# Hash attention and gated feed-forward on one core: the first batch issued from one written list

## The chip, the cores and the metric

The kernel runs on one core of one Trainium2 chip. TensorE (PE) does matrix products, VectorE (DVE) and ScalarE (ACT) do elementwise work and may read PSUM, GpSimd (POOL) does elementwise work on SBUF only, SyncE (SP) issues most of the DMAs. The metric is the device time of one execution in microseconds; less is better. The profile gives a span, from the first to the last instruction of one profiled execution, and that execution's own time.

## The reference

Four batches of eight heads, 768 tokens, head size 64. Each token of q and of k gets a bucket from the signs of six projections; a query attends only to keys in its own bucket. The attention output of a batch (768 tokens x 512) goes through a gated feed-forward layer.

```python
q_bits = (np.einsum('bhsd,dk->bhsk', q, proj) > 0)      # six bits per token, k alike
mask = q_bucket[:, :, :, None] == k_bucket[:, :, None, :]
scores = np.where(mask, scale * q @ k.T, -1e9)
attn = exp(scores - max) / (sum + 1e-9);  x = attn @ v  # 4 x 768 tokens, 512 wide
g = x @ w_gate;  val = x @ w_val
out = x + sigmoid(x @ w_res) * ((gelu(g) * val) @ w_out)
```

## The kernel before, in words

Work goes by *pairs* of heads, four pairs to a batch, sixteen in all (pair 0 to 15). For a pair and a side (0 is q, 1 is k), a tile `ld` holds 12 token groups of 128 tokens (six of either head) by 64 values; the code calls these groups stripes where it handles fewer than six. The path of one side of a pair is:

- `load` or `load_head` (DMA, issued on SP), `tr` (DVE, 32x32 block transposes into `t32`), and `cast` (POOL or ACT, to bf16 in `nat`).
- the hash: for pair 0 `hash_one` (two fp32 matmuls for one head) and `bits_one` (DVE, a transpose and a threshold); for the later pairs `hash_mm` (fp32 matmuls, two or four jobs side by side), `hash_tok` (DVE, one transpose into `ht`) and `bits` (thresholds of 32 partitions each, on DVE or partly on POOL). The six signs stand in `nat` beside the values, so that a plain product of q and k with these 71 rows gives the score with the mask in it.
- the turn to 71 x 128: in batch 0 `turn_pe` (six PE transposes into PSUM) and `turned` (a copy to `aug`); in later batches `turn`, a transposing DMA.
- `vals_a` and `vals_s` (POOL): v in bf16 with a column of ones, and its sum over the token groups.

The attention of a pair is nine *slots*. `scores` makes 1024 columns of scores in one of two PSUM buffers `sp` (1024 columns on PE, L384) and one exponential of 128x1024 on ACT (L389) into one of four `e` buffers. `values`, two slots later (LAG), multiplies `e` by v in eight small matmuls (L358). Slots 0 to 3 and half of slot 4 are the first head of the pair. At the end of a head a `preset` matmul adds a tiny multiple of the sum of v (L330), and `finish` (DVE) divides into `x_tok`. Then x is transposed into `x_sb`, by DMA for pairs 0 and 1 of batch 0, by PE (`x_turn`) for pairs 2 and 3.

After the 36 slots of a batch, `gate_val` runs twelve steps m: product with w_gate, product with w_val (L403, two `sp` buffers), gelu on ACT (L420), product of both on DVE (L423). Its first three quarters of m=0 (`begun`) can start before the last pair is there. `project` (the residual gate and w_out, L435 and L449) is spread over the slots of the next batch, so batches 1 to 3 have feed-forward matmuls to fill PE in their slots and batch 0 has none.

Order is written by hand (`manual_schedule`): each engine executes its instructions in the order in which the program issues them, and waits only for what it needs. The loop over slots issues, for slot s: the scores, the pieces in `side_pe[s]`, the values of slot s-2, then the pieces in `side_work[s]`. Pieces are filed under slots by `at`, `pe`, `turns_pe`, `hash_pe` and `loads`, and under steps of `gate_val` by `gv`. POOL also issues the weight loads (`load_w`), SP the loads of q, k and v, the transposing DMAs and the stores.

Where the change and the prediction touch it: the start of pair 0 (L461 to L487), the fillings of batch 0 (L541 to L572), the next batch's hashes (`hashed`, L517; for pairs 4 and 5 of batch 1 it runs in three quarters before and one quarter inside step m=0, L638 and L639; for pairs 6 and 7 in step m=6, L596; in the later batches half before and half inside m=0, L646 and L647), and the `e` buffers (L388).

## Time and profile before

| what | us |
|---|---|
| three runs | 346.02 to 346.23, median 346.22 |
| the profiled execution: its own time | 346.3 |
| its span | 344.6 |
| stretch 0 to 7.9 (start): PE busy | 6.38 of 7.90 |
| stretch 7.9 to 47.1 (slots of batch 0): PE, ACT, DVE, POOL busy | 37.47, 33.85, 30.37, 33.20 of 39.20 |
| stretch 47.1 to 83.2 (`gate_val` of batch 0): PE busy | 35.73 of 36.10 |
| stretch 83.2 to the end: PE busy | 255.56 of 261.40 |

The stretches come from the view that gives each engine's busy time between two moments. Busy times of PE include the latency of each matmul, so that a chain of matmuls that follow one another with short waits still looks full; what a step costs PE is read from one start to the next. A row of the timeline is: start, duration, engine, line, operation, output<-input, shape, count, and in brackets the idle time before it with what ended it. A row of the groups ends with busy time, mean duration in ns, and the idle time before, with its releaser.

### The profile page before, as it was taken

What the parts mean: (1) busy time and instruction counts of PE and PEld (TensorE: products, weight loads), DVE (VectorE), ACT (ScalarE), POOL (GpSimd) and SP (SyncE); (2) the same over time, 40 slices, a digit from 0 to 9 for tenths busy, and PEclk for the clock granted to TensorE, in tenths of its full rate; (3) what the DMA queues carried; (4) which work ended last, traced back from release to release, by engine and by line L of the source; (5) the groups of instructions that cost most, each with busy time, mean ns of one, the idle gap of its engine ahead of it and who ended that gap; (6) DMA issues with size and microseconds to landing.
All of it is one profiled execution on the core that took longest, in us unless ns stands there. A gap on an engine that the chain in (4) does not pass through costs nothing.

```text
span 344.6 us, 7573 instructions
## 1 busy us (share of the span) xinstructions
PE 335.1 (97%) x3076; PEld 204.8 (59%) x3124; DVE 192.0 (56%) x405; ACT 206.9 (60%) x232; POOL 86.2 (25%) x162
## 2 busy tenths in 40 slices
PE   8999999999999999999999999999999999999996
PEld 5667665655666665655566665656566665555444
DVE  7877757755344866657344684657344444434343
ACT  3889973226999962224999983222899994322220
POOL 4779940343055000260044200143020000000000
PEclk9999999999999999999999999999999999999999
DMA  7939999969476832527466632724420040000012
GB/s 216 374 73 239 243 269 200 158 85 218 132 166 186 219 107 67 103 48 137 93 187 196 216 101 86 137 49 91 91 79 32 32 101 30 30 3 0 32 61 92
DMA packets 71251, 42.90 MB, mean 124 GB/s; under 512 B 49456, under 2 KB 68272, under 8 KB 71216
## 3 DMA queue, kind: packets, MB, share of 16 engines
q1 hardware_dynamic: 64800, 37.17, 42.3%
q0 software_dynamic: 6336, 5.24, 10.1%
q8 instruction: 24, 0.39, 0.4%
q14 instruction: 11, 0.09, 0.1%
q10 hardware_dynamic: 80, 0.00, 0.0%
HBM read 29.36 MB, written 6.29 MB: 103 GB/s over the span
## 4 chain that ended last, share of the span: by engine, by line
PE 88%; ACT 4%; DVE 2%; DMA 2%; issue 2%; SPq 1%; POOL 0%; DVEq 0%; ACTq 0%
PE sp L403 36%; PE fps L449 17%; PE sp L384 15%; PE av L358 8%; PE rps L435 6%; ACT e L389 4%; PE hs L205 3%; DMA ld<-in_k_dram 2%; PE pt L259 1%; DVE o L455 1%; DVE nat L224 0%; SPq L96 0%; DVE o L452 0%; DVE ht L215 0%; PE av L333 0%
## 5 line engine op out<-in xcount | busy, mean ns | idle before, releaser
L389 ACT ACTIVATE e<-sp 128x1024 bf16<-128x1024 f32 x144 | 143.7, 1027 | 13.8 <-PE sp L384 8.2
L420 ACT ACTIVATE gt<-sp 128x768 bf16<-128x768 f32 x48 | 38.9, 811 | 93.0 <-PE sp L403 93.0
L384 PE MATMUL sp<-aug,aug 71*128 71x256 bf16 (+1 forms) x384 | 86.1, 325 | 1.1 <-ACT e L389 0.6
L449 PE MATMUL fps<-wo,hh 128*128 128x512 bf16 (+2 forms) x286 | 74.7, 361 | 1.6
L423 DVE TENSOR_TENSOR hh<-gt,sp 128x768 bf16<-128x768 bf16 x48 | 45.8, 954 | 50.4 <-PE sp L403 45.2
L403 PE MATMUL sp<-x_sb,wg 128*128 128x256 bf16 (+1 forms) x373 | 70.4, 324 | 0.7
L403 PE MATMUL sp<-x_sb,wv 128*128 128x512 bf16 (+1 forms) x379 | 70.6, 325 | 0.4 <-DVE hh L423 0.2
L358 PEld LDWEIGHTS <-e 128*128 128x128 bf16 x1152 | 53.3, 97 | 28.9 <-issue 1.2
L358 PE MATMUL av<-va,e 128*128 128x65 bf16 x1152 | 58.7, 193 | 0.1
L403 PEld LDWEIGHTS <-wv 128*128 128x128 bf16 x384 | 37.5, 98 | 25.1 <-issue 0.3
L403 PEld LDWEIGHTS <-wg 128*128 128x128 bf16 x384 | 36.6, 98 | 26.3 <-issue 3.0
L449 PEld LDWEIGHTS <-hh 128*128 128x128 bf16 x312 | 28.1, 97 | 22.3 <-issue 0.5
L452 DVE SCALAR_TENSOR_TENSOR o<-th,fps 128x512 f32<-128x512 f32 (+2 forms) x26 | 16.8, 645 | 35.9 <-PE fps L449 31.4
L384 PEld LDWEIGHTS <-aug 71*128 71x128 bf16 x384 | 29.4, 97 | 10.9 <-issue 2.1
L184 POOL TENSOR_SCALAR nat<-ld 128x768 bf16<-128x768 f32 (+1 forms) x16 | 14.6, 912 | 76.6 <-DMA aug<-nat 73.2
L281 POOL TENSOR_TENSOR v<-ldv 128x384 f32<-128x384 f32 x16 | 16.0, 1001 | 66.3 <-DMA ldv<-in_v_dram 66.1
L194 DVE STREAM_TRANSPOSE t<-ld 128x768 f32<-128x768 f32 (+1 forms) x34 | 30.9, 914 | 0.9 <-DMA ld<-in_q_dram 0.7
L337 DVE COPY av<-av 128x390 f32<-128x390 f32 x24 | 13.6, 567 | 29.4 <-PE av L333 29.4
L435 PE MATMUL rps<-wr,x_sb 128*128 128x512 bf16 x90 | 25.3, 378 | 0.2
L439 ACT ACTIVATE th<-rps 128x512 f32<-128x512 f32 x24 | 14.2, 593 | 18.5 <-PE rps L435 18.5
L224 DVE TENSOR_SCALAR nat<-htp 32x72 bf16<-32x72 f32 x96 | 21.9, 229 | 1.7
L455 DVE SCALAR_TENSOR_TENSOR o<-o,x_tok 128x512 f32<-128x512 f32 (+2 forms) x26 | 18.4, 709 | 0.9
(61 smaller groups left out, 190.5 us busy)
## 6 DMA issues: line engine op xcount, KB each, us to landing
ldv<-in_v_dram SPq DMA_DIRECT2D x16, 384.0 KB, 5.3
out_dram<-o SPq DMA_DIRECT2D x23, 256.0 KB, 2.0
ld<-in_q_dram SPq DMA_DIRECT2D x15, 384.0 KB, 5.3
ld<-in_k_dram SPq DMA_DIRECT2D x15, 384.0 KB, 6.2
wg<-in_moe_w_gate_dram POOLq DMA_DIRECT2D x4, 384.0 KB, 7.8
wv<-in_moe_w_val_dram POOLq DMA_DIRECT2D x4, 384.0 KB, 9.7
wo<-in_moe_w_out_dram POOLq DMA_DIRECT2D x3, 512.0 KB, 6.3
wr<-in_moe_w_res_dram POOLq DMA_DIRECT2D x1, 512.0 KB, 12.6
```

The costliest lines, as they stand in the source:

```text
L194: nc.vector.transpose(t32[p, side][:, sl].rearrange("p c h n -> p (c h n)"), raw[p, side][:, sl].rearrange("p c d -> p (c d)"))
L224: engs[a % len(engs)].tensor_scalar(nat_of(x)[32 * a:32 * a + 32, :, D:D + NBITS], ht[32 * j:32 * j + 32, :, NBITS * a:NBITS * (a + 1)], 0 ...
L358: nc.tensor.matmul(av[p, hi][:, qt, :], e[:, off:off + P], va[:, hi, jt, 0:D + 1], start=first, stop=(p >= HP and jt == T - 1), skip_group ...
L384: nc.tensor.matmul(sp[:, off:off + nq * P], ks[0:KA, hi * T + jt, :], qs[0:KA, hi * T + qt0:hi * T + qt0 + nq, :], start=True, stop=True)
L389: nc.scalar.activation(e, sp, AF.Exp, scale=float(ALPHA))
L403: nc.tensor.matmul(sp[:, c0:c1], w[:, kk, bass.ts(m, P)], xs[:, kk, c0:c1], start=(kk == 0), stop=(kk == KM - 1))
L420: nc.scalar.activation(gt, sp[:, 0:S], AF.Gelu)
L423: nc.vector.tensor_mul(hidden[b][:, m, :], gt, ps[1][:, 0:S])
L435: nc.tensor.matmul(rps, x_sb[b][:, kk, t, :], wr[:, kk, :], start=(kk == 0), stop=(kk == KM - 1))
L449: nc.tensor.matmul(fps[:, cs], hh[:, m, bass.ts(t, P)], wo[:, m, cs], start=(m == 0), stop=(m == KF - 1))
L452: nc.vector.scalar_tensor_tensor(o[:, cs], th[:, cs], 1.0, fps[:, cs], op0=ALU.add, op1=ALU.mult)
L455: nc.vector.scalar_tensor_tensor(o3, o3, 0.5, x_tok[b][:, k0:k1, t, :], op0=ALU.mult, op1=ALU.add)
```

## The change

Batch 0 no longer runs through the slot loop. A list `PLAN` names every step of it in order, one engine's instruction order being what the list gives that engine. `('S', c)` is the scores and exponential of slot c, `('V', c)` its values, `('w',)` a weight load, `'v'`, `'s'`, `'p'` stand for DVE, ACT and POOL. `BESIDE` and `BESIDE_GV` do the same for the steps beside `gate_val` of batch 0. What differs in the order:

- Pair 0 is hashed, turned and copied in runs of stripes (k 0 to 2, q 0 to 4, q 4 to 6, k 2 to 6, then the second heads whole). Three of the copies ahead of the first exponential, and the copy of the second head's q behind the third, are on ACT. The eight warming matmuls stand together, and the two short ones that stood between the first transposes are gone.
- The exponentials of batch 0 go into a ring of nine, in place of four buffers, and the values are placed by the list, not two slots behind.
- The loads of pair 1 stand ahead of the first v; later loads, casts and thresholds have new places (the thresholds of pair 3's q are all on POOL).
- The hash of pairs 2 and 3 runs in one piece after S12. The hash of pairs 4 and 5 moves from behind the slots to S34 and S35 (three quarters and one quarter). The hash of pairs 6 and 7 moves from step m=6 into step m=0.
- The first part of `gate_val` (`gv` 0) stands after the last values, where before it stood ahead of them.
- Tokens that `hash_tok` writes to SBUF leave a gap of one group after every four, so `bits` reads them as 3 x 4 x 6 in place of 12 x 6.
- In batches 1 and 2 the hash runs whole inside step m=0.

```diff
+PLAN = [
+    ('load', 1, 0), ('load', 1, 1), ('load_v', 0), ('load', 2, 0), ('load_v', 1), ('load', 2, 1),
+    ('load', 3, 0), ('proj', 's', 'pssp'), ('cast', 0, 1, 'p', 0, 6), ('cast', 0, 0, 'p', 6, 12),
+    ('proj', 'w', 'pppp'), ('fill', 1, 256), ('tr', 0, 0, 0, 4), ('cast', 0, 0, 's', 0, 6), ('fill', 7),
+    ('hash1', 0, 0, 0, 4, 'av'), ('tr', 0, 0, 4, 6), ('tr', 0, 1, 2, 6), ('tr', 0, 1, 0, 2),
+    ('cast', 1, 0, 'p'), ('hash1', 0, 1, 0, 2, 'av'), ('tr', 0, 0, 6, 12), ('bits1', 0, 0, 0, 4),
+    ('hash1', 0, 1, 2, 6, 'w1'), ('hash1', 0, 0, 4, 6, 'w0'), ('bits1', 0, 1, 0, 2),
+    ('cast', 0, 1, 'p', 6, 12), ('turn', 0, 1, 0, 2, 'f'), ('load', 3, 1), ('bits1', 0, 1, 2, 6),
+    ('copy', 0, 1, 0, 2, 's'), ('load_v', 2), ('turn', 0, 0, 0, 4, 'r'), ('hash1', 0, 0, 6, 12, 'av'),
+    ('bits1', 0, 0, 4, 6), ('copy', 0, 0, 0, 4, 's'), ('tr', 0, 1, 6, 12), ('bits1', 0, 0, 6, 12),
+    ('cast', 1, 1, 'p'), ('turn', 0, 1, 2, 6, 'f'), ('va', 0), ('turn', 0, 0, 4, 6, 'r'),
+    ('copy', 0, 0, 4, 6, 's'), ('copy', 0, 1, 2, 6, 'v'),
+    ('S', 0), ('tr', 1, 0), ('turn', 0, 0, 6, 12, 'av'),
+    ('S', 1), ('load', 5, 0), ('hash1', 0, 1, 6, 12, 'av'),
+    ('S', 2), ('tr', 1, 1), ('bits1', 0, 1, 6, 12), ('vs', 0), ('cast', 2, 0, 'p'), ('tr', 2, 0),
+    ('copy', 0, 0, 6, 12, 's'),
+    ('S', 3), ('hash', (1,), 0), ('vs', 1), ('hash', (1,), 1), ('hash', (1,), 2),
+    ('turn', 0, 1, 6, 12, 'f'), ('copy', 0, 1, 6, 8, 'v'), ('hash', (1,), 3), ('V', 0), ('load_v', 3),
+    ('S', 4), ('tokens', (1,)), ('copy', 0, 1, 8, 12, 'v'), ('va', 2),
+    ('S', 5), ('V', 1), ('load', 4, 1), ('V', 2), ('V', 3), ('bits', 1, 0, 'v'),
+    ('S', 6), ('bits', 1, 1, 'v'), ('va', 1), ('turn', 1, 0, 0, 6, 'r'), ('tr', 3, 0), ('V', 4),
+    ('S', 7), ('turn', 1, 1, 0, 6, 'f'), ('cast', 2, 1, 'p'), ('copy', 1, 0, 0, 6, 'v'), ('V', 5),
...
+    ('S', 11), ('load_v', 4), ('V', 9), ('copy', 1, 1, 6, 12, 'v'),
+    ('S', 12), ('hash', (2, 3), 0), ('hash', (2, 3), 1), ('hash', (2, 3), 2), ('hash', (2, 3), 3),
+    ('va', 3),
+    ('S', 13), ('load', 5, 1), ('finish', 0, 1), ('tokens', (2, 3)),
+    ('S', 14), ('w',), ('bits', 2, 0, 'vvvp'), ('V', 10), ('V', 11), ('load', 4, 0),
+    ('bits', 2, 1, 'pv'), ('w',), ('turn', 2, 0, 0, 6, 'r'),
+    ('S', 15), ('copy', 2, 0, 0, 6, 'v'), ('V', 12), ('turn', 2, 1, 0, 6, 'f'), ('cast', 3, 1, 'p'),
+    ('bits', 3, 0, 'p'),
+    ('S', 16), ('cast', 3, 0, 'p'), ('copy', 2, 1, 0, 6, 'v'), ('V', 13), ('tr', 5, 0),
+    ('S', 17), ('turn', 2, 1, 6, 12, 'f'), ('load', 7, 1), ('cast', 4, 1, 'p'), ('V', 14),
...
+    ('S', 19), ('bits', 3, 1, 'pv'), ('V', 16),
+    ('S', 20), ('V', 17), ('turn', 3, 0, 0, 6, 'r'), ('load', 6, 1),
+    ('S', 21), ('load', 6, 0), ('V', 18), ('w',),
+    ('S', 22), ('tr', 5, 1), ('turn', 3, 1, 0, 6, 'f'), ('V', 19), ('copy', 3, 0, 0, 6, 'v'),
...
+    ('S', 34), ('va', 4), ('hash', (4, 5), 0), ('hash', (4, 5), 1), ('hash', (4, 5), 2),
+    ('S', 35), ('hash', (4, 5), 3), ('V', 32), ('V', 33), ('tr', 6, 0), ('V', 34), ('tr', 7, 0),
+    ('V', 35), ('gv', 0), ('finish', 3, 1), ('preset', 4, 0), ('tr', 7, 1), ('xturn', 3),
+    ('tokens', (4, 5)), ('gv', 1), ('repeat', 4, 0), ('gelu',), ('load_v', 6),
+]
+BESIDE = [('hash', (6, 7), 0), ('hash', (6, 7), 1), ('hash', (6, 7), 2), ('hash', (6, 7), 3)]
...
-            ht = sm_pool.tile([P, HT, 32], FP32, tag="ht", name="ht")
...
+            ht = hh_pool.tile([P, 3, HT // 3 + 1, 32], FP32, tag="ht", name="ht")[:, :, 0:HT // 3]
...
-    def hash_one(p, side, hi, pool, tag):
+    def hash_one(p, side, c0, c1, tag):
...
-    def turn_pe(p, side, hi, tag=None, pool=mm_ps):
+    def turn_pe(p, side, c0, c1, tag, pool=mm_ps):
...
-        e = e_pool.tile([P, 1024], BF16, tag="e", name="e")
+        if p < HP:
+            if c == 0 and p == 0:
+                ring.append(hh_pool.tile([P, NE, 1024], BF16, tag="hh", name="ering"))
+            e = ring[0][:, (p * NCH + c) % NE]
+        else:
+            e = e_pool.tile([P, 1024], BF16, tag="e", name="e")
...
+    for m, name, *args in BESIDE_GV:
+        gv(0, m, lambda name=name, args=args: STEP[name](*args))
+    for name, *args in PLAN:
+        STEP[name](*args)
+    gate_val(0, begun, lambda: [STEP[name](*args) for name, *args in BESIDE])
+    mlp.append(project(0))
...
-                    hashed(ps, 0, 2)
-                    gate_val(b, begun, lambda: hashed(ps, 2, 4))
+                gate_val(b, begun, lambda: hashed(ps))
```

233 lines of the change are left out of this document (101 added, 132 removed), and 16 rows, old and new, of the table PLAN.

## The prediction

> **What bounds the kernel now.** The page comes first: PE is called busy for nearly all of the span, so anything that is to help must take work or waiting off PE.
>
> ```profile
> span 344.6 us, 7573 instructions
> PE 335.1 (97%) x3076; PEld 204.8 (59%) x3124; DVE 192.0 (56%) x405; ACT 206.9 (60%) x232; POOL 86.2 (25%) x162
> ```
>
> That share is an average and includes latency, so I went on to the groups of the stretch 8 to 47, the slots of batch 0, and to ACT's timeline there.
>
> ```profile
> L389 ACT ACTIVATE e<-sp 128x1024 bf16<-128x1024 f32 x36 | 34.5, 1025 | 5.6 <-PE sp L384 5.3
> ```
>
> ```profile
> 8.58 4.08 ACT L389 ACTIVATE e<-sp 128x1024 bf16<-128x1024 f32 x4 [0.89 <-PE sp L384]
> 13.65 1.02 ACT L389 ACTIVATE e<-sp 128x1024 bf16<-128x1024 f32 x1 [1.00 <-PE sp L384]
> ...
> 37.26 10.46 ACT L389 ACTIVATE e<-sp 128x1024 bf16<-128x1024 f32 x11 [0.16 <-PE sp L384]
> 47.73 1.28 ACT L633 ACT_TABLE_LOAD   x1
> ```
>
> The 36 exponentials start at 8.58 and end at 47.72 (37.26 + 10.46). ACT stood still for 5.6 us before them, 0.89 of it ahead of the first; so some 4.7 us between the first and the last are ACT waiting for scores. In an unbroken run one exponential follows the other after 10.46 / 11 = 0.951.
>
> What a slot costs PE is read from starts:
>
> ```profile
> 6.35 0.50 PE L259 MATMUL pt<-ident,nat 128*71 128x128 bf16 x6 [0.46 <-DVE nat L242]
> 6.68 0.38 PE L150 MATMUL wps<-warm 128*128 128x256 bf16 x2
> ...
> 7.24 0.87 PE L234 MATMUL hs<-t,projs 128*128 128x192 f32 x4
> 7.94 0.60 PE L384 MATMUL sp<-aug,aug 71*128 71x512 bf16 x2
> ...
> 17.16 0.60 PE L384 MATMUL sp<-aug,aug 71*128 71x256 bf16 x3
> 17.60 0.41 PE L358 MATMUL av<-va,e 128*128 128x65 bf16 x8
> 17.85 0.60 PE L384 MATMUL sp<-aug,aug 71*128 71x512 bf16 x3
> ```
>
> Scores 0.44, values 0.25, together 0.69; the turn of a head's side 0.33; one head's hash for pair 0 0.70. Against ACT's 0.951, PE has 0.26 a slot for turns, hashes and presets. The two are close, so a hash in one piece starves ACT, and waiting for ACT idles PE. Behind the slots PE runs without a break; there a microsecond less of PE work is a microsecond of the total.
>
> ```profile
> 48.08 0.41 PE L358 MATMUL av<-va,e 128*128 128x65 bf16 x8
> 48.33 0.33 PE L330 MATMUL av<-vsum,eps_sb 128*128 128x390 bf16 x1
> 48.50 1.14 PE L403 MATMUL sp<-x_sb,wv 128*128 128x512 bf16 x6
> 49.54 0.51 PE L342 MATMUL pt<-ident,x_tok 128*128 128x128 bf16 x6
> 49.98 1.18 PE L205 MATMUL hs<-t,projw 128*32 128x192 f32 x24
> 51.10 0.50 PE L403 MATMUL sp<-x_sb,wg 128*128 128x512 bf16 x2
> ...
> 51.85 0.53 PE L205 MATMUL hs<-t,projw 128*32 128x192 f32 x8
> 52.49 1.46 PE L403 MATMUL sp<-x_sb,wg 128*128 128x512 bf16 x7
> ```
>
> ```profile
> 68.18 1.51 PE L205 MATMUL hs<-t,projw 128*32 128x192 f32 x32
> 69.62 1.47 PE L403 MATMUL sp<-x_sb,wg 128*128 128x512 bf16 x7
> ```
>
> From these: a preset 0.17, six matmuls of the first gate part 1.04, three quarters of a four-job hash 1.12 (49.98 to 51.10), the last quarter 0.64 (51.85 to 52.49), a whole one 1.44. Step m=1 starts at 52.49, which is 4.77 behind the last exponential.
>
> **The change part by part.** All sums are against the profiled execution, 346.3 us by its own time, which lies 0.1 above the median of the runs, 346.22.
>
> *The start.* Now and after, the thresholds of pair 0 stand on DVE behind the transpose of q's second head, and that waits for its DMA:
>
> ```profile
> 5.12 0.58 DVE L194 STREAM_TRANSPOSE t<-ld 128x384 f32<-128x384 f32 x1 [0.71 <-DMA ld<-in_q_dram]
> 5.62 0.35 DVE L240 STREAM_TRANSPOSE hs<-hs 128x192 f32<-128x192 f32 x1
> ...
> 6.12 0.39 DVE L240 STREAM_TRANSPOSE hs<-hs 128x192 f32<-128x192 f32 x1
> ```
>
> So the chain begins at 5.62 as before. A threshold pair of 192 columns takes 0.50 (5.62 to 6.12); I put 128 columns at 0.43 and 64 at 0.36, so k's first two stripes are ready at about 6.5 and PE's turns start at 6.63 (the same 0.14 behind as the row at 6.35). Then two turns and four (0.33), the second head's hash (0.70), four and two more (0.33): scores 0 at 8.0, against 7.94. The first exponential waits for the three copies on ACT and starts at 8.65 to 8.7, 0.1 late. The eight stripe matmuls in place of four cost between the same column time and twice a pair's 0.70 again (1.4); they run while DVE waits for the DMA, so I take 0, and 0.5 at the far end. Dropping the two short warming matmuls gives PE their time back where it now waits for DVE: nothing.
>
> *Slots 0 to 4.* After scores 0 PE does: turn of q's second head, which waits for DVE to about 8.6; scores 1 to 9.4; hash 0.70; scores 2 to 10.5; scores 3, when exponential 1 is done, to 11.1; three of pair 1's four hash quarters 1.12; a turn 0.33; the last quarter about 0.5; values 0; scores 4 to 13.9. With 0.17 to drain, exponential 4 starts at 14.05 against 13.65: 0.4 late. The copy that ACT has behind exponential 2 (0.8) lies in that wait and costs nothing; without the wait it would cost 0.75.
>
> *Slots 4 to 35.* Nine buffers in place of four cost nothing in time; PE can leave values for later. Where there are only turns (0.33) and presets (0.17) between scores, PE's 0.69 + 0.33 in one slot and 0.69 in the next keep ahead of 2 x 0.951. Three places do not: two values, a turn, a value and a preset ahead of S11 (0.15 late); the whole hash ahead of S13, where PE, less than half a slot ahead, spends 1.44 + 0.43 + 0.17 (0.75); three quarters of a hash ahead of S35 (0.45). So the last exponential ends at 14.05 + 31 x 0.951 + 1.03 + 1.35 = 45.9, against 47.72: **-1.8**. The ends: no gap at all, -3.2; every gap as large as now, +0.4.
>
> *From there to step m=1.* A load of 384 KB takes this long from its issue, here k of pair 1:
>
> ```profile
> L78 SPq DMA_DIRECT2D ld<-in_k_dram x1: 469/469/469, 3.7 to 3.7; - x1
> ...
> DMA to landing us min/median/max: 6.5/6.5/6.5
> ```
>
> Last values and preset 0.49, then the first gate part 1.04, which now stands behind the values and so covers `finish`; the transposes of x, 1.56 to their use as now (49.54 to 51.10), with the second gate part inside; two short products 0.75; the hash of pairs 6 and 7 1.44. With 0.03 for the preset of pair 4 that is 5.3 against 4.77: **+0.55**. The transpose `tr` of pair 7's q stands ahead of the last `finish` on DVE; if its load were late, the last x would be late with it. SP issues that load behind the transposing DMA of pair 1's x, near 36 (pair 1's last `finish` near 33); with 6.5 it lands by 43, and DVE comes to it near 45.
>
> *Step m=6* loses its hash: **-1.44** (68.18 to 69.62); pairs 4 and 5 were hashed in the 1.8 that the slots now take in.
>
> *Batches 1 and 2*: one whole hash (1.44) in place of two halves.
>
> ```profile
> 130.51 0.79 PE hs L205 x16
> ...
> 132.05 0.79 PE hs L205 x16
> ```
>
> 2 x 0.79 - 1.44 = 0.14 each: **-0.28**. What can be lost here is cover for the transposing DMA of the last x, since the product that needs it moves 0.8 forward; at most 1.6 for both.
>
> *DVE, POOL and the queues.* ACT takes four copies off DVE; DVE has room. POOL has not: from the cast of pair 1's k to the thresholds of pair 3's k it has six casts, four `va`, two `vs`, five weight loads and nine thresholds.
>
> ```profile
> 17.03 0.82 POOL L273 CAST va<-ldv 128x768 bf16<-128x768 f32 x1
> ...
> 17.85 0.81 POOL L186 CAST nat<-ld 128x768 bf16<-128x768 f32 x1
> 18.64 1.00 POOL L281 TENSOR_TENSOR v<-ldv 128x384 f32<-128x384 f32 x1
> ...
> 20.71 0.84 POOL L184 TENSOR_SCALAR nat<-ld 128x768 bf16<-128x768 f32 x1
> ```
>
> ```profile
> L224 POOL TENSOR_SCALAR nat<-ht 32x72 bf16<-32x72 f32 x6 | 2.9, 481 | 3.7 <-DVE ht L215 3.3
> L169 POOL DMA_DIRECT2D wg<-in_moe_w_gate_dram x4 | 3.4, 852 | 0.1
> ```
>
> A cast is 0.79 and a `va` 0.82 (next start), a `vs` 2.07, a weight load 0.85, a threshold 0.48: 4.7 + 3.3 + 4.1 + 4.3 + 4.3 = 20.7. Pair 1's k lands at 10.2 now (3.7 + 6.5); it moves ahead of the first v on SP and lands no later, I take 9.2. With about one us of waits for later loads POOL is through at 31, and PE wants pair 3's k at about 31.6: just in time, cost 0. The gap in the hash results changes the access of these thresholds; no row shows it. Ends: none, or each as dear as POOL's larger operation, 0.83 (row at 20.71), nine times 0.35 = 3.2.
>
> *A rule against it.* Six thresholds on DVE took 1.30 with POOL waiting or doing the same, and 2.16 at 28.62 while POOL did its adds:
>
> ```profile
> 25.36 1.30 DVE L224 TENSOR_SCALAR nat<-ht 32x72 bf16<-32x72 f32 x6
> ...
> 28.62 2.16 DVE L224 TENSOR_SCALAR nat<-ht 32x72 bf16<-32x72 f32 x6
> ```
>
> Pair 1's eight thresholds now run beside POOL's `vs` 1, ahead of the copies that S9 needs, and S9 has no slack: by the row at 28.62 they cost 8 x 0.14 = 1.2 more. I take 0, since the gapped access is new and the row at 25.36 is as near, and keep 1.2 as a rival. The Trainium skill, "SBUF — State Buffer", section "SBUF: two separate sides", says that DVE (in its faster modes) and GpSimd share one pair of ports and whoever starts first keeps the pair for the whole instruction. The two rows agree with it; by that rule the sum would be about 1.2 us less of a gain.
>
> Sum: -1.8 + 0.55 - 1.44 - 0.28 = **-3.0**, so 346.2 - 3.0 = **343.2**.
>
> **The rivals.**
> 1. *Ports*: as above, one exponential run broken at S9, 1.2 us lost: 344.4. For it the row at 28.62; against it, PE is itself late by S13 and part of the loss falls into that gap.
> 2. *PE was full already*: the 97% is right, ACT's waits are only PE's work seen from ACT, and moved hashes cost in the slots what they save behind them. Only the fp32 switches are saved: 346.2 - 0.28 = 345.9. For it, the page; against it, the starts: 36 x 0.69 = 24.8, fifteen turns 5.0, eight presets 1.4 and the hashes (0.7 and twice about 1.5) make 35 of the 39 us that lie before 47.1.
> 3. *POOL sets the pace, and it is slower.* The place is the turns of pair 3. At a threshold of 0.83 POOL is 3.2 late there, less 0.6 of room: 345.8. From about 0.88 on it decides; at the 1.0 of POOL's adds (row at 18.64) it is 4.7 late, less 0.6, and S22 to S35 follow: 343.2 + 4.1 = 347.3. For it: POOL's list is full without a break. Against it: 0.48 is what the same work took without the gap.
> 4. *Cover lost in batches 1 and 2*: the 1.6 above: 344.8.
>
> **How the numbers follow.** The forecast has 0.53; its own range is 341.4 (neither the three gaps of 1.35 nor the 0.4 at exponential 4) to 344.2 (the start 0.5 late, and one more gap of half the row at 13.65). Rivals 1 and 4 together 0.19, rival 2 0.09, rival 3 0.19. A measurement of this kernel can tell about 0.2% (0.7 us) from no change. Faster by more: forecast and rivals 1 and 4, 0.72; within: rival 2, 0.09; slower: rival 3, 0.19. The range reaches from 341.4 to 346.4: it takes in all but rival 3.
>
> **What would show it.** Right: exponential 4 at about 14, then runs on ACT broken only ahead of S11, S13 and S35; the last one ends at 45.9; m=1 starts at 51.2; no L270 row in m=6; one x32 hash each in batches 1 and 2. Wrong: POOL's thresholds above 0.5, PE's turns (L331) waiting for POOL, DVE's thresholds stretched near 15, exponentials waiting between S21 and S28, or PE waiting for a DMA of x_sb near 127.

## The result, and the profile after

| kernel | us, median (range) | ratio to the kernel before | 95% interval |
|---|---|---|---|
| before, in the same rounds | 346.12 (345.89 to 346.23) | 1 | |
| after the change | 344.56 (343.73 to 344.80) | 0.9952 | 0.9933 to 0.9970 |

The change makes the kernel about 1.6 us faster; forecast were 3.0. The profiled execution after took 344.8 by its own time, with a span of 343.1 (before: 346.3 and 344.6).

The groups of ACT in the whole span, and ACT's timeline in the slots of batch 0, after the change:

```profile
L467 ACT ACTIVATE ering<-sp 128x1024 bf16<-128x1024 f32 x36 | 34.7, 1026 | 2.6 <-PE sp L457 2.2
```

```profile
8.87 1.02 ACT L467 ACTIVATE ering<-sp 128x1024 bf16<-128x1024 f32 x1
10.16 2.11 ACT L467 ACTIVATE ering<-sp 128x1024 bf16<-128x1024 f32 x2 [0.26 <-PE sp L457]
...
14.65 8.79 ACT L467 ACTIVATE ering<-sp 128x1024 bf16<-128x1024 f32 x9 [0.78 <-PE sp L457]
24.16 19.17 ACT L467 ACTIVATE ering<-sp 128x1024 bf16<-128x1024 f32 x20 [0.72 <-PE sp L457]
43.55 1.94 ACT L467 ACTIVATE ering<-sp 128x1024 bf16<-128x1024 f32 x2 [0.22 <-PE sp L457]
45.72 1.02 ACT L467 ACTIVATE ering<-sp 128x1024 bf16<-128x1024 f32 x1 [0.23 <-PE sp L457]
```

ACT's idle time ahead of the exponentials went from 5.6 to 2.6. The runs without a break are long now: nine exponentials from 14.65, twenty from 24.16. The last one ends at 46.74 (before: 47.72).

PE behind the slots, after the change:

```profile
47.22 1.14 PE L481 MATMUL sp<-x_sb,wg 128*128 128x512 bf16 x6
48.20 0.19 PE L407 MATMUL av<-vsum,eps_sb 128*128 128x65 bf16 x1
49.34 0.51 PE L416 MATMUL pt<-ident,x_tok 128*128 128x128 bf16 x6 [0.94 <-DVE x_tok L378]
...
51.51 1.51 PE L270 MATMUL hs<-t,projw 128*32 128x192 f32 x32
52.95 1.47 PE L481 MATMUL sp<-x_sb,wg 128*128 128x512 bf16 x8
```

Step m=1 starts at 52.95, later than the 52.49 of before: the 0.98 won at the last exponential and more (1.44) are lost in the six microseconds behind it. Some 0.55 of that was forecast; 0.94 is one wait of PE for the last x. DVE's timeline and the chain of waits say where that comes from:

```profile
47.63 0.98 DVE L259 STREAM_TRANSPOSE t<-ld 128x768 f32<-128x768 f32 x1 [2.85 <-DMA ld<-in_q_dram]
...
48.72 0.56 DVE L378 TENSOR_TENSOR x_tok<-av,rec 128x384 bf16<-128x384 f32 x1
```

```profile
34.76 0.78 SPq L385
...
36.35 11.18 DMA ld<-in_q_dram
```

Pair 7's q was issued at 36.35, right behind the transposing DMA of pair 1's x, and landed 11.18 later. Its transpose holds DVE's queue for 2.85 us, and the last `finish` stands behind it.

From step m=1 to the end it took 290.15 us (343.1 - 52.95) against 292.1: 1.96 less. So the total is +0.46 up to m=1 and -1.96 from there, -1.5. The second figure is the less sure: in ten other traces below (all but the ring of four) the same stretch, with the same code, took 289.3 to 290.0. Below, edits to batch 0 are therefore compared by the way to m=1 as well as by the times.

### The profile page after: what moved, and what is told of

It is laid out like the page before. It is cut to its first block, busy times and chain, and to the rows that moved or that the text cites. A ratio compares the mean times of both kernels' runs of the same rounds, so it can differ in the third digit from the quotient of the medians.

```text
span 343.1 us, 7640 instructions
## 1 busy us (share of the span) xinstructions
PE 337.0 (98%) x3130; PEld 206.4 (60%) x3130; DVE 190.3 (55%) x406; ACT 207.9 (61%) x235; POOL 87.0 (25%) x165
## 4 chain that ended last, share of the span: by engine, by line
PE 92%; DMA 3%; DVE 3%; issue 0%; SPq 0%; POOL 0%; DVEq 0%; POOLq 0%
PE sp L481 36%; PE fps L527 18%; PE sp L457 16%; PE av L432 9%; PE rps L513 6%; DMA ld<-in_q_dram 3%; PE hs L270 3%; PE pt L331 1%; PE wps L215 1%; DVE o L533 1%; PE hs L305 1%; DVE o L530 0%; DVE t L259 0%; DVE x_tok L378 0%; PE av L407 0%
## 5 line engine op out<-in xcount | busy, mean ns | idle before, releaser
L467 ACT ACTIVATE e<-sp 128x1024 bf16<-128x1024 f32 x108 | 109.2, 1027 | 8.3 <-PE sp L457 2.8
L527 PE MATMUL fps<-wo,hh 128*128 128x512 bf16 (+2 forms) x312 | 79.6, 363 | 0.0
L481 PE MATMUL sp<-x_sb,wg 128*128 128x512 bf16 (+1 forms) x384 | 70.9, 326 | 0.0
L432 PEld LDWEIGHTS <-e 128*128 128x128 bf16 x864 | 40.3, 97 | 25.1
L432 PE MATMUL av<-va,e 128*128 128x65 bf16 x864 | 43.4, 193 | 0.0
L467 ACT ACTIVATE ering<-sp 128x1024 bf16<-128x1024 f32 x36 | 34.7, 1026 | 2.6 <-PE sp L457 2.2
L249 POOL TENSOR_SCALAR nat<-ld 128x768 bf16<-128x768 f32 (+1 forms) x16 | 13.8, 865 | 77.3 <-DMA aug<-nat 72.8
L259 DVE STREAM_TRANSPOSE t<-ld 128x768 f32<-128x768 f32 (+3 forms) x36 | 31.0, 871 | 3.8 <-DMA ld<-in_q_dram 3.5
L513 PE MATMUL rps<-wr,x_sb 128*128 128x512 bf16 x96 | 27.1, 379 | 0.0
L291 DVE TENSOR_SCALAR nat<-htp 32x72 bf16<-32x72 f32 x80 | 18.3, 228 | 1.5
## 6 DMA issues: line engine op xcount, KB each, us to landing
wr<-in_moe_w_res_dram POOLq DMA_DIRECT2D x1, 512.0 KB, 11.2
```

Source lines behind the costliest of these rows:

```text
L259: nc.vector.transpose(t32[p, side][:, sl].rearrange("p c h n -> p (c h n)"), raw[p, side][:, sl].rearrange("p c d -> p (c d)"))
L291: engs[a % len(engs)].tensor_scalar(nat_of(x)[32 * a:32 * a + 32, :, D:D + NBITS], ht[32 * j:32 * j + 32, ..., NBITS * a:NBITS * (a + 1)], ...
L432: nc.tensor.matmul(av[p, hi][:, qt, :], e[:, off:off + P], va[:, hi, jt, 0:D + 1], start=first, stop=(repeats(p, hi) and jt == T - 1), ski ...
L467: nc.scalar.activation(e, sp, AF.Exp, scale=float(ALPHA))
L481: nc.tensor.matmul(sp[:, c0:c1], w[:, kk, bass.ts(m, P)], xs[:, kk, c0:c1], start=(kk == 0), stop=(kk == KM - 1))
L513: nc.tensor.matmul(rps, x_sb[b][:, kk, t, :], wr[:, kk, :], start=(kk == 0), stop=(kk == KM - 1))
```

## The experiments

Each had its own runs of the kernel before beside it, so the ratios compare best.

| edit | us, median | ratio | 95% interval |
|---|---|---|---|
| load of pair 7's q earlier | 343.42 | 0.9922 | 0.9909 to 0.9935 |
| hash results without gaps | 345.21 | 0.9964 | 0.9949 to 0.9979 |
| pair 0 by whole heads | 345.07 | 0.9971 | 0.9961 to 0.9981 |
| early load, and pairs 4 and 5 hashed behind the slots | 343.95 | 0.9939 | 0.9927 to 0.9951 |
| early load, and whole heads | 343.69 | 0.9927 | 0.9913 to 0.9941 |
| early load, and no gaps | 344.33 | 0.9947 | 0.9930 to 0.9964 |
| early load, and ring of four | 356.74 | 1.0292 | 1.0254 to 1.0331 |
| early load, and no warming matmuls | 344.64 | 0.9955 | 0.9944 to 0.9967 |
| early load, and the hash of pairs 4 and 5 spread | 343.61 | 0.9922 | 0.9910 to 0.9935 |
| early load, and ring of five | 343.59 | 0.9929 | 0.9915 to 0.9943 |
| late load, last `finish` ahead of its transpose | 343.93 | 0.9935 | 0.9923 to 0.9947 |

**The late load.** One step is moved in the list.

```diff
-    ('S', 21), ('load', 6, 0), ('V', 18), ('w',),
+    ('S', 21), ('load', 6, 0), ('load', 7, 0), ('V', 18), ('w',),
...
-    ('S', 30), ('V', 27), ('cast', 5, 1, 'p'), ('V', 28), ('load', 7, 0), ('tr', 6, 1),
+    ('S', 30), ('V', 27), ('cast', 5, 1, 'p'), ('V', 28), ('tr', 6, 1),
```

> One step moved in the list: the load of pair 7's q is issued by SP right behind that of pair 6's q (near S21, about 24 us) and not behind the transposing DMA of pair 1's x (36.35 us). Theory (the late load): in the changed kernel its transpose on DVE at 47.63 waited 2.85 us for the landing, the last finish stood behind it, and PE waited 0.94 us for x_tok at 49.34. With the load landed by 40 (it took 11 to 13 us from issues near 24 to 28) that wait is gone: step m=1 starts at about 52.0 in place of 52.95 and the time falls by 0.8 to 1.0, to 343.6 to 343.8. Rival (something else is late there, for instance the last values or the first gate part, which stand ahead of the same place on PE): the wait only changes its name, m=1 stays at 52.9 and the time at 344.6. Against both: an earlier load may delay the loads beside it (pair 6's, landing in 11 to 14 us), which would show as waits of DVE between 36 and 44.

Measured: 343.42, by the ratios 0.3% or 1.0 us faster than the changed kernel; the two intervals only just touch, so the trace has to show it. PE behind the slots with the early load:

```profile
47.48 0.33 PE L404 MATMUL av<-vsum,eps_sb 128*128 128x390 bf16 x1
47.65 1.14 PE L481 MATMUL sp<-x_sb,wg 128*128 128x512 bf16 x6
48.62 0.19 PE L407 MATMUL av<-vsum,eps_sb 128*128 128x65 bf16 x1
48.69 0.51 PE L416 MATMUL pt<-ident,x_tok 128*128 128x128 bf16 x6
```

The wait is gone, and nothing took its place: from the end of the values' preset to the transposes of x PE has no gap. Step m=1 came at 52.31, not 52.0, because in this execution exponential 4 came 0.40 later (15.05; the start, below). From exponential 4 to m=1 it took 37.26 in place of 38.30: 1.04 less. No wait of DVE for a DMA is seen between 36 and 44. The theory holds, with a time a little below the 343.6 to 343.8 expected, though the load was not as early as expected: SP, which works through its queue in order, issued it at 31.0, not near 24, and it took 12.5, so it landed at 43.5. That was early enough. This version is 2.7 us, or 0.78%, faster than the kernel before.

**The order on DVE alone.** The load stays late; the transpose that needs it goes behind `finish`.

```diff
-    ... ('V', 34), ('tr', 7, 0),
-    ('V', 35), ('gv', 0), ('finish', 3, 1), ('preset', 4, 0), ...
+    ... ('V', 34),
+    ('V', 35), ('gv', 0), ('finish', 3, 1), ('tr', 7, 0), ('preset', 4, 0), ...
```

> The load of pair 7's q stays late, as in the changed kernel, but on DVE its transpose now stands behind the last finish in place of ahead of it. Theory (PE's wait of 0.94 us came from the order on DVE, not from the landing as such): PE gets the last x at about 48.4 whatever the load does; where it lands at 47.5 the transpose is done by 48.9, ahead of need, and the time is 343.4 to 343.8; where it lands near 49, as in two other executions, the copy of the transposed x behind it is late by up to 1. So 343.4 to 344.2. Rival (the hash of pairs 6 and 7 needs that transpose soon after, so the late landing is paid all the same): 344.4 to 344.7.

Measured: 343.93, by the ratios 0.6 us faster than the changed kernel, with intervals that overlap; the trace has to decide again. PE gets the last x at 48.42 with no wait, and then waits for what now stands behind the transposes on DVE, the copy of the transposed x (PE, then DVE, with the late load and the new order):

```profile
48.42 0.51 PE L416 MATMUL pt<-ident,x_tok 128*128 128x128 bf16 x6
48.76 1.14 PE L481 MATMUL sp<-x_sb,wv 128*128 128x512 bf16 x6
50.75 0.48 PE L481 MATMUL sp<-x_sb,wg 128*128 128x512 bf16 x2 [0.85 <-DVE x_sb L419]
```

```profile
48.55 1.84 DVE L259 STREAM_TRANSPOSE t<-ld 128x768 f32<-128x768 f32 x2 [0.19 <-DMA ld<-in_q_dram]
50.31 0.39 DVE L419 COPY x_sb<-pt 128x512 bf16<-128x512 bf16 x1
```

Here the load landed at about 48.5, a microsecond later than in the trace of the changed kernel; in the other two runs with the late load (no gaps, whole heads) it landed in time for transposes at 49.13 and 48.92. With the list's own order PE came to the last x 1.70 to 1.71 behind the start of that transpose in three traces, and to the second gate part 1.43 or 1.44 later (two traces). By these rows a transpose at 48.55 would have put the second gate part at 51.69, an estimate; with `finish` first it came at 50.75, 0.94 earlier. From exponential 4 to m=1 it took 38.15, only 0.15 less than in the changed kernel, because the load was so much later here. So both the landing and the place in DVE's queue belong to the cause, and the order alone takes away only a part. From its issue the load took 11.2 to 12.3 in the four traces with the late load, and 1.5 us lie between the earliest and the latest landing; in the changed kernel's order all of that is paid. Why it takes so long there was not tried.

**Whole heads in place of stripes**, for pair 0, first with the late load, then with the early one. The steps of the two runs are the same; the core of the edit:

```diff
-    ('hash1', 0, 0, 0, 4, 'av'), ('tr', 0, 0, 4, 6), ('tr', 0, 1, 2, 6), ('tr', 0, 1, 0, 2),
-    ('cast', 1, 0, 'p'), ('hash1', 0, 1, 0, 2, 'av'), ('tr', 0, 0, 6, 12), ('bits1', 0, 0, 0, 4),
-    ('hash1', 0, 1, 2, 6, 'w1'), ('hash1', 0, 0, 4, 6, 'w0'), ('bits1', 0, 1, 0, 2),
...
+    ('hash1', 0, 0, 0, 6, 'av'), ('tr', 0, 1, 0, 6),
+    ('cast', 1, 0, 'p'), ('hash1', 0, 1, 0, 6, 'av'), ('tr', 0, 0, 6, 12), ('bits1', 0, 0, 0, 6),
...
+    ('copy', 0, 0, 0, 6, 's'), ... ('copy', 0, 1, 0, 2, 'v'), ('copy', 0, 1, 2, 6, 'v'),
```

> Pair 0 is hashed, turned and copied by whole heads, as in the kernel before, in place of stripes; the rest of the list is that of the changed kernel. Theory (the stripes cost time): with them PE's sixteen fp32 records took 4.23 to 6.95 where eight took 4.24 to 5.89, DVE's second pair of thresholds waited 0.31 for them, the first exponential came at 8.87 against 8.58 and exponential 4 at 14.65 where 14.05 was forecast. Without stripes the first exponential starts at 8.5 to 8.6 and exponential 4 at 14.1 to 14.4; the time falls by 0.3 to 0.6, to 344.0 to 344.3. Rival (what is late at exponential 4 is pair 1's hash, 1.69 us of PE between S3 and S4, whatever the stripes do): the first exponential moves by up to 0.3 and exponential 4 stays at 14.5 to 14.7; time 344.4 to 344.7. Third (stripes help, since scores need less of the keys at first): exponential 4 later than 14.7 and the time up to 0.4 above the changed kernel's.

Measured: 345.07, nearest the third case by the time, the rival by the trace: exponential 4 at 14.56, and then PE waits 2.33 for the last x, since the load landed late. That run could not decide, so it was made again with the early load.

> Pair 0 by whole heads again, now with the early load of pair 7's q as well, so that the late landing can't hide the difference; to be compared with the run that has the early load alone (343.42). In the first run by heads exponential 0 came at 8.76 and exponential 4 at 14.56, in four runs by stripes at 8.76 to 9.28 and 14.23 to 15.05. Theory now (stripes are neutral here: what they gain in order they lose in sixteen weight loads in place of eight, and exponential 4 hangs on pair 1's hash): the time is within 0.3 of 343.4, exponential 4 at 14.2 to 14.6. Rival (stripes cost 0.3 to 0.6): 342.9 to 343.1. Third (stripes gain): 343.8 or more.

Measured: 343.69 against 343.42, intervals that overlap nearly whole: no difference to be told. Exponential 4 came at 15.05, outside the 14.2 to 14.6 expected, because the second head's q landed late in this execution (5.81, below). What sets the first exponential is seen over all traces with warming matmuls. DVE's row of the second head's q, and behind it PE's stripe records (the sixteen fp32 matmuls that hash the stripes), in the changed kernel:

```profile
5.30 0.58 DVE L259 STREAM_TRANSPOSE t<-ld 128x384 f32<-128x384 f32 x1 [0.70 <-DMA ld<-in_q_dram]
```

```profile
4.23 1.81 PE L305 MATMUL hs<-t,projs 128*128 128x128 f32 x8
5.83 1.12 PE L305 MATMUL wps<-t,projs 128*128 128x128 f32 x8
```

and the same two with the early load, then with the early load and no gaps, and DVE's row alone for whole heads with the early load:

```profile
5.23 0.58 DVE L259 STREAM_TRANSPOSE t<-ld 128x384 f32<-128x384 f32 x1 [0.70 <-DMA ld<-in_q_dram]
```

```profile
4.24 1.81 PE L305 MATMUL hs<-t,projs 128*128 128x128 f32 x8
5.84 1.52 PE L305 MATMUL wps<-t,projs 128*128 128x128 f32 x8
```

```profile
5.61 0.58 DVE L259 STREAM_TRANSPOSE t<-ld 128x384 f32<-128x384 f32 x1 [1.10 <-DMA ld<-in_q_dram]
```

```profile
4.24 1.01 PE L305 MATMUL hs<-t,projs 128*128 128x128 f32 x8
5.08 1.06 PE L305 MATMUL wps<-t,projs 128*128 128x128 f32 x8
```

```profile
5.81 0.58 DVE L257 STREAM_TRANSPOSE t<-ld 128x384 f32<-128x384 f32 x1 [1.37 <-DMA ld<-in_q_dram]
```

The first exponentials came at 8.87, 9.28, 9.15 and 9.24. By whole heads it comes 3.43 to 3.46 behind the start of that DVE transpose (three traces, the kernel before among them). By stripes it comes 3.54 behind it where PE's sixteen records are through by 6.6 (5.61 + 3.54 = 9.15), and otherwise 1.92 behind the end of the records: 6.95 + 1.92 = 8.87, 7.36 + 1.92 = 9.28. So at the first exponential stripes cost 0.1 where PE is quick, and up to 0.6 where it is slow. What the rest of the batch starts from is exponential 4. Counted from the start of the same DVE transpose it comes 9.24 later by whole heads in this list (two traces), and by stripes 9.01 or 9.02 later where PE is quick (four traces) and 9.35 to 9.82 where it is slow (five traces). So there stripes win 0.2 in the one case and lose 0.1 to 0.6 in the other, which fits two times that can't be told apart. Both the landing (5.08 to 5.81) and PE's pace (the second row ends between 6.1 and 7.4) vary from execution to execution.

**No warming matmuls.**

```diff
-    ('proj', 'w', 'pppp'), ('fill', 1, 256), ('tr', 0, 0, 0, 4), ('cast', 0, 0, 's', 0, 6), ('fill', 7),
+    ('proj', 'w', 'pppp'), ('tr', 0, 0, 0, 4), ('cast', 0, 0, 's', 0, 6),
```

> The eight warming matmuls are left out, with the early load; to be compared with the run that has the early load alone. In five runs with them the first hash records on PE had weight loads of 0.33 us up to a moment between 4.1 and 6.9 us and 0.19 from then on, with a granted clock of 1.00 throughout. Theory (PE runs at a lower rate until it has been busy for 3 to 6 us): without matmuls ahead of 4.2 all sixteen stripe records take 0.216 each (3.5 in all, to 7.7), the turns behind them are slow as well, the first exponential comes at 9.8 to 10.5 and the time rises by 0.6 to 1.5, to 344.0 to 344.9. Rival (the slow weight loads are something else, for instance DMA traffic into SBUF, and the warming does nothing): records as before, the first exponential at 8.8 to 9.3 and the time at 343.4.

Measured: 344.64, by the ratios 1.1 more than with them; the first exponential came at 10.31. PE's timeline without them:

```profile
4.04 1.94 PE L305 MATMUL hs<-t,projs 128*128 128x128 f32 x8 [4.04 <-DVE t L259]
5.78 1.92 PE L305 MATMUL wps<-t,projs 128*128 128x128 f32 x8
7.48 0.85 PE L331 MATMUL pt<-ident,nat 128*71 128x128 bf16 x6
8.12 1.38 PE L305 MATMUL hs<-t,projs 128*128 128x192 f32 x4
9.34 0.50 PE L331 MATMUL pt<-ident,nat 128*71 128x128 bf16 x6
```

All sixteen records are slow, and so are the first turn (0.85 against 0.50 at 9.34) and the second head's hash (1.38 against 0.87). PE reaches its full pace near 9.2, between the last slow weight load at 8.9 and the turn at 9.34, some 5 us behind its first matmul. The theory holds.

**The gap in the hash results**, with the late load and with the early one.

```diff
-            ht = hh_pool.tile([P, 3, HT // 3 + 1, 32], FP32, tag="ht", name="ht")[:, :, 0:HT // 3]
+            ht = hh_pool.tile([P, 3, HT // 3, 32], FP32, tag="ht", name="ht")
```

> Only the gap in the tile of the hash results is taken out; all else is the changed kernel. Theory (the gap is what spares DVE the wait for POOL): in the kernel before, six thresholds on DVE took 2.16 us beside POOL's adds (0.36 each, row at 28.62); in the changed kernel eight took 1.83 (0.23 each, row at 14.69) beside the same adds at 13.73 to 15.7. Without the gap the eight go to 2.6 to 2.9, pair 1's copies and S9 come up to 0.8 late, and the time rises by 0.4 to 1.0, to 345.0 to 345.6. Rival (where the adds fall was chance, and the gap does nothing): the eight stay at 1.8 to 1.9 and the time at 344.6 within 0.2. Third: the gap costs something by itself; then the kernel without it is faster, and POOL's thresholds (0.48 to 0.51 each) become shorter.

> The tile of the hash results without gaps, with the early load; to be compared with the run that has the early load alone (343.42). In the first run without gaps fifteen thresholds on DVE took 281 ns each in place of 217, pair 1's eight 2.20 us in place of 1.83, two beside POOL's adds 1.05 in place of 0.46; from exponential 4 to the last end ACT took 32.4 us in place of 32.1. Theory (the gap saves DVE about 1 us of waits, of which 0.3 reaches the scores): 343.6 to 343.9. Rival (all of it is hidden by room on DVE): 343.4 within 0.15. If DVE's eight again take 2.2 and the two 1.05, that the gap does this doesn't hang on one execution.

Measured: 345.21 with the late load, where PE's wait for the last x (2.54 in the profiled execution) hides the matter, and 344.33 with the early load, 0.9 above the early load alone and 0.4 over the range expected (single executions from 343.43 to 345.46). DVE's thresholds up to 35 us as a group, and pair 1's eight in the timeline, first with gaps (the changed kernel), then without (with the early load):

```profile
L291 DVE TENSOR_SCALAR nat<-ht 32x72 bf16<-32x72 f32 x15 | 3.3, 217 | 0.3
```

```profile
14.69 1.83 DVE L291 TENSOR_SCALAR nat<-ht 32x72 bf16<-32x72 f32 x8
```

```profile
L291 DVE TENSOR_SCALAR nat<-ht 32x72 bf16<-32x72 f32 x15 | 5.1, 340 | 0.3
```

```profile
14.67 3.14 DVE L291 TENSOR_SCALAR nat<-ht 32x72 bf16<-32x72 f32 x8
```

Pair 1's eight take 3.14 without gaps (0.39 each), and ACT's run breaks close to S9, where the prediction's first rival had put it (ACT, early load without gaps):

```profile
14.63 3.92 ACT L467 ACTIVATE ering<-sp 128x1024 bf16<-128x1024 f32 x4 [0.78 <-PE sp L457]
19.11 1.02 ACT L467 ACTIVATE ering<-sp 128x1024 bf16<-128x1024 f32 x1 [0.56 <-PE sp L457]
20.48 1.95 ACT L467 ACTIVATE ering<-sp 128x1024 bf16<-128x1024 f32 x2 [0.35 <-PE sp L457]
```

Exponentials 8 and 9 wait 0.56 and 0.35. In the run with the late load the same eight took 2.20, less than the 2.6 to 2.9 expected, and ACT's run broke by 0.16 only, ahead of S11; there POOL was idle from 15.8 to 17.8, where in the run with the early load it began casts at 16.85 while DVE's eight still ran. So by these two traces what is lost without gaps depends on the POOL work that happens to fall beside the thresholds. The gap is what keeps DVE out of POOL's way: with it the fifteen take 217 ns in the mean, though the same adds run on POOL. Beside POOL's own thresholds nothing is lost either way: five on DVE took 1.16 with gaps (24.20) and 1.16 to 1.20 without. POOL's thresholds are 452 ns with or without.

**The moved hash of pairs 4 and 5**, put back behind the slots, with the early load.

```diff
-    ('S', 34), ('va', 4), ('hash', (4, 5), 0), ('hash', (4, 5), 1), ('hash', (4, 5), 2),
-    ('S', 35), ('hash', (4, 5), 3), ('V', 32), ('V', 33), ...
+    ('S', 34), ('va', 4),
+    ('S', 35), ('V', 32), ('V', 33), ...
...
+    ('hash', (4, 5), 0), ('hash', (4, 5), 1), ('hash', (4, 5), 2), ('hash', (4, 5), 3), ('tr', 7, 1),
...
-    t32_pool = ctx.enter_context(tc.tile_pool(name="t32", bufs=6))
+    t32_pool = ctx.enter_context(tc.tile_pool(name="t32", bufs=7))
```

> The early load as in the run with that edit, and beside it the hash of pairs 4 and 5 (1.44 us of PE) put behind the last transposes of x, out of the slots of batch 0; one more buffer for the transposed q and k, which that order needs. To be compared with the run that has the early load alone. Theory (PE had time to spare in the slots, so the moved hash was mostly hidden): in the changed kernel it showed ahead of S34 and S35 as gaps of 0.22 and 0.23 on ACT. Taken out, the last exponential ends 0.3 to 0.5 earlier, 1.44 is paid behind it, and the time is 0.9 to 1.2 above that of the early load alone. Rival 2 of the prediction (PE was full already, what is moved only shifts): the time is the same within 0.2. In between, half the gain from the hash taken out of step m=6 (1.44) was paid in the slots.

Measured: 343.95, 0.5 to 0.6 above the early load alone, where the theory had 0.9 to 1.2. Counted from exponential 4, so that the start plays no part, the way to step m=1 took 38.33 (52.77 - 14.44) against 37.26: 1.07 more. PE, and behind it ACT, show the room:

```profile
46.25 0.42 PE L433 MATMUL av<-va,ering 128*128 128x65 bf16 x8 [0.49 <-ACT ering L468]
```

```profile
43.34 2.85 ACT L468 ACTIVATE ering<-sp 128x1024 bf16<-128x1024 f32 x3 [0.22 <-PE sp L458]
```

Without the hash PE waits 0.49 for the last exponential; with it there is no such wait. ACT's gap ahead of S35 (0.23 to 0.24 with the hash) is gone, but the 0.22 ahead of S33 is still there, so that one is not the hash's. From exponential 4 to the end of the last one it took 31.75, against 32.11 with the hash. So of the 1.44 about 1.1 is hidden in the slots, and 0.4 is paid there. By the trace the theory holds; the times alone would fit the half-way case as well.

**Spread thinner.**

```diff
-    ... ('cast', 5, 1, 'p'), ('V', 28), ...
+    ... ('cast', 5, 1, 'p'), ('hash', (4, 5), 0), ('V', 28), ...
-    ('S', 33), ('finish', 3, 0), ('open', 4, 0),
-    ('S', 34), ('va', 4), ('hash', (4, 5), 0), ('hash', (4, 5), 1), ('hash', (4, 5), 2),
+    ('S', 33), ('finish', 3, 0), ('open', 4, 0), ('hash', (4, 5), 1),
+    ('S', 34), ('va', 4), ('hash', (4, 5), 2),
```

> With the early load, two quarters of the hash of pairs 4 and 5 are moved forward: one behind values 27 (S30), one behind S33, in place of three in one piece behind S34; to be compared with the run that has the early load alone (343.42). In the changed kernel's trace PE waited for a free score buffer by 0.23, 0.07, 0.20 and 0.07 us between 37.6 and 41, while at the end the three quarters left ACT gaps of 0.22 and 0.23. Theory (PE has idle time in S28 to S33 and none at the end, so what is filled there is won): the two gaps ahead of exponentials 33 and 35 go, the last exponential ends about 0.4 earlier, step m=1 comes 0.3 to 0.5 earlier, and the time is 342.9 to 343.1. Rival (the idle time is needed, and each quarter there makes a gap of its own): the gaps only move, and the time is 343.4 within 0.2. With a share of DVE in it (the transposes of pair 4's k come late and the quarter waits for them) it would be up to 0.5 slower.

Measured: 343.61, the same as without. The rival was right: the gaps only moved. ACT has 0.17 ahead of S31 and 0.16 ahead of S33, where the early load alone has 0.22 ahead of S33 and 0.24 ahead of S35. From exponential 4 to m=1 it took 37.35 against 37.26. The trace also shows a cost that the rival did not name, since the pieces take longer than the whole (PE, start to next start):

```profile
40.27 0.53 PE L270 MATMUL hs<-t,projw 128*32 128x192 f32 x8
40.74 0.42 PE L432 MATMUL av<-va,ering 128*128 128x65 bf16 x8
...
43.72 0.53 PE L270 MATMUL hs<-t,projw 128*32 128x192 f32 x8
44.18 0.61 PE L457 MATMUL sp<-aug,aug 71*128 71x256 bf16 x3
```

A quarter alone takes 0.46 to 0.47; four alone are 1.87 where three quarters and one are 1.11 + 0.46 = 1.57 and one whole is 1.44. So the two extra breaks in the hash took about 0.3 (1.87 against 1.57), the least that the theory hoped to win; that it is the change between fp32 and bf16 matmuls that costs this is only inferred.

**The ring.** First four places in place of nine, then five.

```diff
-    NE = 9
+    NE = 4
```

> The ring of exponentials has four places in place of nine, with the early load; to be compared with the run that has the early load alone. The list puts the values of slot 10 behind the scores of slot 14, so with four places exponential 14 can't start before values 10 are through. Theory (the prediction's: nine places cost nothing in time and let PE leave values for later, which matters only at the hash of pairs 2 and 3): exponential 14 waits for values 10, which PE does right behind scores 14, so that 0.2 to 0.6 is lost there, and the time is 343.5 to 344.0. Rival (the ring carries the gain): exponentials wait in many slots and 1.5 or more is lost, 344.9 or more.

With four places the values of slots 1, 10 and 20 to 23 read a later slot's exponentials, as they are issued behind the scores that write the place again. They wait for these (356.74), and the run says nothing on the ring.

> Five places in the ring in place of nine, with the early load; to be compared with the run that has the early load alone (343.42). In the run with four places the list wrote a place again before its values had been issued wherever values come four slots late (slots 1, 10 and 20 to 23), so those values took a later slot's exponentials: another computation, whose time says nothing on the question. Five places are the fewest that the list allows. Theory (the prediction's term of 0 for the ring): the values that free a place stand on PE ahead of the scores that need it, so no exponential waits, and the time is 343.4 within 0.2. Rival (the ring's size matters): exponentials 15 and 25 to 28, whose place is freed one slot before, come late by 0.2 or more each, and the time is 344.0 or more.

Measured: 343.59, the same as nine places. From exponential 4 to the end of the last one it took 32.18 against 32.11. The theory holds; the list needs five places, and the other four win no time.

## Why the prediction was right or wrong

The time, 344.56, lies in the range, between the forecast of 343.2 and no change. By the number alone it is nearer to rivals 1 (344.4) and 4 (344.8), but the traces show neither of them. The direction and the mechanism (hashes off the stretch where PE is full, into slots with room) were right; of the 1.5 that are missing, 0.9 lie in one wait behind the slots and 0.8 ahead of it, and 0.2 came back later.

- *The start*: forecast 8.65 to 8.7, measured 8.87. The chain behind DVE's transpose was sized right (5.12 + 3.54 = 8.66). Here that transpose started at 5.30, 0.18 later, and that is nearly all of the difference: 5.30 + 3.54 = 8.84. The stripe records, put at 0 with 0.5 at the far end, took 2.7; DVE waited 0.31 for them, but the first exponential came only 0.03 later for it. In the trace with the early load they cost 0.5 (5.23 + 3.54 = 8.77, measured 9.28), the far end.
- *Slots 0 to 4*: exponential 4 at 14.65, forecast 14.05, so the 0.4 was 1.0. Of the 0.6 too much, 0.2 is the start. The other 0.4 goes from exponential 0 to 4: 5.78 where the forecast had 5.4. In the four traces by stripes, with warming, where PE's records did not hold DVE up it took 5.47 or 5.48, so 0.3 of this goes with PE's slow start.
- *Slots 4 to 35*: 31.07 from exponential 4 to exponential 35, forecast 30.83. The gap ahead of S13 is 0.72 (forecast 0.75), that ahead of S35 is 0.23 (0.45), that ahead of S11 isn't there (0.15). One of 0.22 ahead of S33 was not forecast; PE does two values and a preset between the scores there, and the gap stays when the hash is taken out. So the gaps add up to 1.17 against 1.35, and that this is near is in part luck. The rest is that an exponential in a run took 0.96 to 0.98, not 0.951. With these terms the last exponential ends at 46.74 in place of 45.9: -0.98, not -1.8.
- *From there to step m=1*, the step that failed: 6.21, forecast 5.3, before 4.77. The order of work was as described, the hash of pairs 6 and 7 took 1.44 (51.51 to 52.95). What was mis-sized is the load of pair 7's q. The prediction named it as what would make the last x late, and then gave it the 6.5 of a load issued at 3.7 us. It took 11.2, and PE waited 0.94 for the last x where the sum had nothing. The trace of before had shown such values for loads issued at this time (its q and k loads between 30 and 50 us):

```profile
L78 SPq DMA_DIRECT2D ld<-in_q_dram x2: 467/520/574, 34.8 to 36.4; - x2
...
DMA to landing us min/median/max: 6.3/9.8/13.3
```

  With the median of these it lands at 46.2 and costs about nothing; with the 13.3 it lands at 49.7, 2.1 later than it did, and the wait is 3 us. With the load early, the same list gave 343.42: the forecast, 0.2 off, and that is luck in part. By that run's trace the last exponential ended 1.26 later than forecast (47.16 against 45.9), the way from there to m=1 was 0.15 shorter, and from m=1 on it was 0.8 less than the terms for step m=6 and batches 1 and 2 make of the trace of before (289.59 against 292.11 - 1.72).
- *Step m=6*: -1.44 forecast; from m=1 to the first scores of batch 1 it took 28.61 in place of 30.14, -1.53. Right.
- *Batches 1 and 2*: -0.14 each forecast; from the first gate part to m=1 it took 6.73 and 6.72 in place of 6.96 and 6.97, -0.24 each. Right in kind, and larger: 0.2 in all. No wait for a DMA of the last x is seen; rival 4 did not come.
- *Ports* (rival 1): the eight thresholds of pair 1 took 0.23 each, near the 0.22 of the row at 25.36. It did not come, and the runs without gaps show why: there they took 0.28 and 0.39, and with the early load ACT lost 1.1 between exponentials 4 and 13 (10.62 against 9.51) and the time 0.9, with the late load ACT only 0.16. The mechanism was right, the 1.2 about its far end, and the gap takes it away. The Trainium skill, "SBUF — State Buffer", section "SBUF: two separate sides", has the pair of ports locked by whichever of DVE (in its faster modes) and GpSimd starts first; the rows without gaps agree with it (0.39 against 0.23). The prediction found that both of its rows agree with that rule. The row at 25.36 doesn't show it: POOL ran two thresholds from 25.50 to 26.55 beside it, and DVE lost nothing. Why POOL's adds and casts slow DVE and its thresholds don't stays open. That the gap brings DVE out of the mode that takes the pair is only inferred.
- *PE was full already* (rival 2): for the hash of pairs 4 and 5 it is so at most to 0.4 of 1.44, by the trace with the hash behind.
- *POOL sets the pace* (rival 3): its thresholds stayed at 0.45 to 0.51, and no exponential between S21 and S28 waits. It did not come. The prediction counted it as slower and outside the range, though its own lower end, 345.8, lies inside the range and below the time before.
- *The ring*: 0, as forecast.

## What to carry to other kernels

A load's time from issue to landing is a matter of place: take it from rows of the same stretch, and take the longest of them when a queue with critical work waits on it, since a wait in an in-order queue is paid by all that stands behind. When an edit wins less than its parts promise, look for the one new wait at the seam between stages; moving one load here won 1.0 us, where the rest of the list had won 1.6. The fp32 hash among bf16 matmuls took 1.44 whole and 1.87 in four pieces, so it was better moved whole than in crumbs.

## What the runs showed of the hardware

PE starts slow and becomes quick at a moment that changes from one execution to the next. The weight loads of the stripe records took 0.33 us up to that moment and 0.19 behind it. Those of the last eight records, with the early load, and then without gaps and with the late load (view of one tile; the three numbers are the shortest, the median and the longest, in ns):

```profile
L305 PEld LDWEIGHTS wps<-t,projs x8: 192/312/333, 5.7 to 7.0; 128*128 128x128 f32 x8
```

```profile
L305 PEld LDWEIGHTS wps<-t,projs x8: 192/193/193, 5.2 to 6.0; 128*128 128x128 f32 x8
```

The moment lay before 4.1 us in the second of these traces, near 5.7 in that of the changed kernel and near 6.7 in the first, with the first matmul at 1.06 in all. The granted clock in the profile's rows was 1.00 all that time, so that row doesn't show it. The Trainium skill, "TensorE: Matmul & The Clock Gate", section "Part 1: The HAM clock gate (the "warmup" mystery)", says that PE runs at half its clock until some 4 us of sustained work, by a window that runs freely, so that the moment varies; these traces agree in kind, with under 3.1 to 5.6 us from the first matmul on, a wider spread than the half microsecond either way that the page gives.

In the run without gaps and with the late load, PE's wait of 2.54 us for the last x was followed by a stretch at a lower granted clock (column before the last two, in the view of stretches):

```profile
47.00:52.00 5.00, 2.30 (x22) 1.45 (x20) 2.70 (x5) 0.59 (x2) 0.00 (x0) 0.96 1.22 270
52.00:56.00 4.00, 4.00 (x40) 1.87 (x39) 2.73 (x8) 2.09 (x3) 0.00 (x0) 0.62 1.26 205
```

That execution took 347.57, the longest of its kernel. With whole heads a wait of 2.33 was followed by no such stretch (1.00). The length of one wait doesn't decide it: with four places in the ring no wait of PE there was over 1.7, and yet the granted clock was 0.50 from 18 to 20, behind a wait of 1.60 that ended at 16.66, and 0.50 again from 45 to 54, behind five microseconds with PE busy for 2.05; behind a wait of 1.66 that ended at 29.54 it stayed at 1.00. So waits of PE can cost again behind themselves; what decides it stays open.

In the profiled execution of the ring of five PE stood still for 0.98 us among the last values, with nothing in the profile that it waited for:

```profile
48.39 0.22 PE L432 MATMUL av<-va,ering 128*128 128x65 bf16 x2 [0.98 <-issue]
```

Its cause stays open; the other traces of these kernels don't have it.
